# Experts' weights loaded by GpSimd instead of SyncE in an attention and mixture-of-experts kernel

## The chip, the cores and the metric

The kernel runs on one core of a Trainium2 chip. A core has five engines that work side by side, each through its own list of instructions in order: TensorE (PE in the profile; its weight loads are shown apart as PEld), VectorE (DVE), ScalarE (ACT), GpSimd (POOL) and SyncE (SP). Engines wait for each other through semaphores. Transfers between the device memory and the core's buffers are issued by an engine into a DMA queue and carried out by 16 DMA engines. The metric is the device time of one execution in microseconds (us), the median of several runs.

## The reference

Eight sequences of 2496 positions go through an attention without a softmax, then all 19968 tokens through a soft mixture of 8 experts with 4 slots each:

```python
scores = (1/S) * z @ z.T                 # per sequence, S = 2496, z: S x 64
x = u * (maximum(scores, 0)**2 @ v)      # u, v: S x 256
logits = x @ phi                         # 19968 x 32
d = softmax of logits over the tokens
slot_in = d.T @ x                        # 32 slots x 256
slot_out[e] = maximum(slot_in[e] @ w1[e], 0) @ w2[e]   # w1: 8 x 256 x 1024, w2: 8 x 1024 x 256
out = (softmax of logits over the slots) @ slot_out
```

The experts' weights, 16.8 MB in all, are needed only when the slot inputs of all tokens have been summed, that is, after the whole attention.

## The kernel before, in words

**Attention.** The work is a list of 410 "halves" (`halves`, line 209). A half is one block of up to 512 queries against two tiles of 128 keys. For each half the kernel needs the squared scores, split into a rounded part `ph` and its remainder `pl`; three matmuls per pair of tiles then add them into `acc`. Since the score matrix is symmetric, many blocks are not computed again: VectorE transposes a block into `y`, SyncE stores it in device memory (`turned`), and later SyncE fetches it as `r` (`fetch`, line 231). The queries of the last sequence end with a block that is cut in two chunks of 256, so the last 20 halves are half as wide as the others. `weights` (line 599) counts the last 30 halves, 380 to 409.

Where the half three places ahead must be computed (not fetched), `sums_halves` (line 354) runs the current half in two phases on the two row groups of TensorE. Between them stands a hand-over: a no-op on GpSimd waits for the last matmul of phase 0, and the first matmul of phase 1 waits for that no-op. TensorE runs the scores of the half ahead between the phases. The no-op is not an instruction that the profile lists.

**Tokens.** While the attention runs, the token groups of 1024 (`groups`, line 447) are worked off in small pieces, one per half: `logits`, exponentials, and a transposition of the tokens. For the last of these, VectorE turns 32 x 32 blocks (`y`), and 16 small DMAs (`shift`, line 441, four calls of four) move them into place in `xt`. `slot_sums` (line 529; `sl` in the profile) then multiplies `xt` by itself on TensorE: the exponentials against the tokens. The last full group, number 18, has its four shifts and its slot sums among the last halves; the last 512 tokens follow after the attention on a path of their own (lines 744 to 845), which uses two small GpSimd results: line 759 clears part of `tiny`, and line 761 prepares a mask.

**Weights.** 32 loads of 512 KB each (`load_w`, line 594) bring in the experts' weights. `weights(i)` issues loads 0 to 21 in a written order among the last 30 halves, into buffers that the attention no longer needs: 16 that held the split `z` and `v` of the last two sequences, and three that held `y` and `r`. Loads 15, 14, 12, 13, 6, 7, 5, 8, 9, 10 and 11 come in the last ten halves, and each needs a buffer that one of these halves still reads. Loads 22 to 31 (lines 739 to 742) go into space that is free when the attention ends. Layer 1 of the experts reads weights 0 to 15, layer 2 weights 16 to 31.

**Order.** The class `InOrder` (line 51) pins each instruction behind the one traced before it on its engine. TensorE, ScalarE, VectorE and SyncE are used through it. GpSimd is not: a planner orders its instructions by the time at which it reckons them ready, those traced first ahead. The planner also chooses which freed buffer a load takes. A DMA waits in its engine's list until its buffer is free, and all that stands behind it on that engine waits too. DMAs of one issuing path rotate over eight semaphores, and a DMA waits for the one eight places before it to land.

Of the kernel before, what the change touches and what calls it, by code (L numbers as in the profile page):

```python
# [62 lines left out]
def attn_soft_moe_kernel(ctx, tc, uT, v, zz, phi, ww, outT):  # L63
    nc = tc.nc

    pe, act, dve, sp = (InOrder(tc, x) for x in (nc.tensor, nc.scalar, nc.vector, nc.sync))

    def pool(st, name, n, side=None):
        return st.enter_context(
# [522 lines left out]
        w_raw.append(pool.tile([P, 2, 512], F32, tag=tag, name=f"w_{len(w_raw)}"))  # L592

    def load_w(i):
        sp.dma_start(w_raw[i], ww[i].rearrange("p (k n) -> p k n", k=2))

    w_raw = []

    def weights(i):

        if i == 0:
            for _ in range(NBLK):
                take_w(blk, "blk")
        if i == 10:
            for _ in range(3):
                t = turns_sb.tile([P, 16, 4, NS], F32, tag="y", name=f"w_{len(w_raw)}")
                t = t.rearrange("p m i q -> p (m i q)").rearrange("p (a k n) -> p a k n", a=2, k=2)
                w_raw.extend([t[:, 0], t[:, 1]])  # L610
        order = [[], [0], [], [1], [], [2], [], [3], [], [4]]
        order += [[], [16], [17], [], [18], [19], [], [20], [21], []]
        order += [[], [15], [14], [12], [13], [6], [7, 5], [8], [9], [10], [11]]
        for k in order[i]:
            load_w(k)
# [124 lines left out]
    for i in range(NBLK + 6, NW):  # L740
        take_w(wx, "wx")
        load_w(i)

    q = NQG - 1
    x = xg_.pop(q)
# [286 lines left out]
```

## Time and profile before

| | |
|---|---|
| median of 3 runs | 1408.99 us (1407.65 to 1409.12) |
| profiled execution | 1410.43 us, its span 1408.7 us |
| busy share of the span: PE, DVE, ACT, POOL | 97%, 77%, 65%, 0% |
| mean granted TensorE clock | 0.976 |
| DMA queues in use by the kernel | one (q1), 271.02 MB |
| loads of weights | 32 of 512.0 KB, median 7.6 us from issue to landing |

The page is made from one execution. Its numbers are microseconds from the first instruction on, if nothing else is said. A row of a timeline gives start, duration, engine, operation, the tile that is written and those that are read, and how often; in brackets stands the idle time of the engine ahead of it and who ended it. A row of the waits gives who waited for whom, the total, how often and the longest. A row of the stretches gives length, then the busy time and number of instructions of PE, PEld, DVE, ACT and POOL, the granted clock, the DMA share and GB/s; where one engine is asked for, only its own busy time stands there. Nearly all instructions carry line 59, since the helper `InOrder` records them; the tiles' names tell them apart. "SPq" is SyncE's queue of DMA issues. The time of an issue is not that of the transfer.

### The profile page before, as it was taken

What the parts mean: (1) busy time and instruction counts of PE and PEld (TensorE: products, weight loads), DVE (VectorE), ACT (ScalarE), POOL (GpSimd) and SP (SyncE); (2) the same over time, 40 slices, a digit from 0 to 9 for tenths busy, and PEclk for the clock granted to TensorE, in tenths of its full rate; (3) what the DMA queues carried; (4) which work ended last, traced back from release to release, by engine and by line L of the source; (5) the groups of instructions that cost most, each with busy time, mean ns of one, the idle gap of its engine ahead of it and who ended that gap; (6) DMA issues with size and microseconds to landing.
All of it is one profiled execution on the core that took longest, in us unless ns stands there. A gap on an engine that the chain in (4) does not pass through costs nothing.

```text
span 1408.7 us, 27263 instructions
## 1 busy us (share of the span) xinstructions
PE 1362.1 (97%) x11029; PEld 1079.7 (77%) x11029; DVE 1085.8 (77%) x1401; ACT 913.8 (65%) x1046; POOL 4.2 (0%) x22
## 2 busy tenths in 40 slices
PE   9899999999999999899999999899999999999885
PEld 6677887778777887688877888688877788778752
DVE  6778797778888698577987788687888879686454
ACT  7766586757767487465867577474876567664353
POOL 0000000000000000000000000000000000000000
PEclk9999999999999999999999999999999999999985
DMA  4236566394676647576675745748476856659889
GB/s 128 68 109 184 183 154 189 118 290 137 170 233 208 230 111 185 155 214 210 159 211 143 285 138 139 220 127 289 122 189 183 268 160 168 194 149 308 300 329 387
DMA packets 106493, 272.74 MB, mean 194 GB/s; under 512 B 14720, under 2 KB 17280, under 8 KB 95104
## 3 DMA queue, kind: packets, MB, share of 16 engines
q1 hardware_dynamic: 106368, 271.02, 63.6%
q8 instruction: 86, 1.41, 0.4%
q14 instruction: 39, 0.32, 0.1%
HBM read 148.41 MB, written 100.14 MB: 176 GB/s over the span
## 4 chain that ended last, share of the span: by engine, by line
PE 83%; DMA 7%; ACT 3%; DVE 3%; issue 2%; SPq 1%; ACTq 0%; DVEq 0%
PE acc L59 65%; PE sc L59 11%; DMA r<-turned 5%; PE lg L59 3%; PE pf L59 2%; SPq L59 1%; DMA xt<-y 1%; ACT r L59 1%; ACT ot L59 1%; DVE pl L59 1%; ACT ph L59 1%; DVE y L59 1%; PE po L59 1%; PE h L59 1%; DVE xg L59 0%
## 5 line engine op out<-in xcount | busy, mean ns | idle before, releaser
L59 PE MATMUL acc<-ph,v 64*128 64x512 f32 (+5 forms) x5092 | 988.3, 387 | 3.9 <-DVE v L59 1.7
L59 PEld LDWEIGHTS acc<-ph,v 64*128 64x128 f32 (+1 forms) x5092 | 600.6, 186 | 150.7 <-issue 19.7
L59 DVE TENSOR_TENSOR pl<-r,ph 128x1024 fp32r<-128x1024 f32 (+1 forms) x412 | 488.3, 1191 | 196.4 <-ACT ph L59 180.8
L59 PE MATMUL acc<-pl,v 64*128 64x512 f32 (+5 forms) x2546 | 624.5, 384 | 1.8 <-DVE pl L59 1.8
L59 ACT CAST ph<-r 128x1024 fp32r<-128x1024 f32 (+1 forms) x259 | 260.7, 1021 | 204.8 <-DMA r<-turned 130.0
L59 ACT ACTIVATE r<-sc 128x1024 f32<-128x1024 f32 (+1 forms) x252 | 254.9, 1012 | 199.9 <-PE sc L59 192.6
L59 PEld LDWEIGHTS acc<-pl,v 64*128 64x128 f32 (+1 forms) x2546 | 308.4, 185 | 62.5 <-DVE pl L59 4.2
L59 ACT ACTIVATE r<-r 128x1024 f32<-128x1024 f32 (+1 forms) x252 | 263.5, 1047 | 7.2
L59 DVE STREAM_TRANSPOSE y<-r 128x1024 f32<-128x1024 f32 x152 | 188.2, 1238 | 0.0
L59 DVE CAST ph<-r 128x1024 fp32r<-128x1024 f32 (+1 forms) x153 | 102.1, 667 | 57.3 <-ACT r L59 56.6
L59 PE MATMUL sc<-z,z 64*128 64x512 f32 x960 | 138.9, 393 | 2.3 <-DVE z L59 1.4
L59 PEld LDWEIGHTS sc<-z,z 64*128 64x128 f32 x960 | 89.9, 184 | 24.9 <-ACT r L59 2.2
L59 PE MATMUL sc<-z 64*128 64x512 f32 (+1 forms) x480 | 68.4, 390 | 0.0
L59 DVE TENSOR_TENSOR v<-vr,v 128x512 fp32r<-128x512 f32 x80 | 54.0, 675 | 3.7 <-ACT v L59 3.7
L59 DVE TENSOR_TENSOR xg<-acc,ut 128x1024 f32<-128x1024 f32 (+7 forms) x57 | 48.6, 875 | 9.0 <-PE acc L59 9.0
L59 DVE STREAM_TRANSPOSE y<-xg 128x512 f32<-128x512 f32 x76 | 52.6, 692 | 2.5 <-DMA xt<-y 2.5
L59 PEld LDWEIGHTS sc<-z 64*128 64x128 f32 x480 | 45.0, 186 | 8.6
L59 ACT CAST v<-vr 128x512 fp32r<-128x512 f32 x80 | 48.8, 610 | 2.2 <-DMA vr<-in_v 2.2
L59 DVE TENSOR_TENSOR z<-zr,z 64x512 fp32r<-64x512 f32 x70 | 48.1, 687 | 2.0
L59 ACT CAST z<-zr 64x512 fp32r<-64x512 f32 x70 | 43.4, 619 | 2.0 <-DMA zr<-in_zz 0.3
L59 DVE COPY ot<-pf 128x1024 f32<-128x1024 f32 (+2 forms) x22 | 24.3, 1104 | 21.7 <-PE pf L59 21.7
L59 ACT COPY ot<-pf 128x1024 f32<-128x1024 f32 (+2 forms) x22 | 20.1, 915 | 25.6 <-PE pf L59 25.6
(128 smaller groups left out, 417.2 us busy)
## 6 DMA issues: line engine op xcount, KB each, us to landing
turned<-y SPq DMA_DIRECT2D x304, 256.0 KB, 4.3
r<-turned SPq DMA_DIRECT2D x72, 1024.0 KB, 7.7
xt<-y SPq DMA_DIRECT2D x304, 72.0 KB, 3.4
vr<-in_v SPq DMA_DIRECT2D x80, 256.0 KB, 2.9
w<-in_w SPq DMA_DIRECT2D x32, 512.0 KB, 7.6
outT<-ot SPq DMA_DIRECT2D x16, 1024.0 KB, 6.3
ut<-in_uT SPq DMA_DIRECT2D x31, 512.0 KB, 4.3
zr<-in_zz SPq DMA_DIRECT2D x35, 256.0 KB, 7.3
```

Of the source, the lines that this page charges most:

```text
L59: return lambda *a, **k: self.tc.keep_in_program_order(f(*a, **k))
```

## The change

`load_w` issues through GpSimd, by a fifth `InOrder`, and no longer through SyncE. The number, size, written order and destinations of the loads stay as they are, and so does everything else. Being pinned, each load stands behind what was traced before it on GpSimd, no-ops and other loads; the no-ops and lines 759 and 761 are not pinned behind the loads.

```diff
-    pe, act, dve, sp = (InOrder(tc, x) for x in (nc.tensor, nc.scalar, nc.vector, nc.sync))
+    engines = nc.tensor, nc.scalar, nc.vector, nc.sync, nc.gpsimd
+    pe, act, dve, sp, pool_q = (InOrder(tc, x) for x in engines)
...
     def load_w(i):
-        sp.dma_start(w_raw[i], ww[i].rearrange("p (k n) -> p k n", k=2))
+        pool_q.dma_start(w_raw[i], ww[i].rearrange("p (k n) -> p k n", k=2))
```

## The prediction

> **What bounds the kernel now.** I read the page's first part, then who waits for whom around the 32 loads, then the timelines of SyncE and TensorE there.
>
> ```profile
> PE 1362.1 (97%) x11029; PEld 1079.7 (77%) x11029; DVE 1085.8 (77%) x1401; ACT 913.8 (65%) x1046; POOL 4.2 (0%) x22
> ```
>
> TensorE (PE) is busy 97% of the span, so a change of queues can only move its idle time. The loads as a group (ns at least, median, at most; first and last start), and all that TensorE waited for between 1255 and 1350 us (total, times, longest):
>
> ```profile
> L59 SPq DMA_DIRECT2D w<-in_w x32: 327/398/1319, 1263.6 to 1341.1; - x32
> ```
>
> ```profile
> PE sl L59 <- DMA xt<-y: 5.7, 1, 5.7
> PE et_sums L59 <- DVE tiny L59: 0.9, 1, 0.9
> PE h L59 <- ACT tiny L59: 0.3, 1, 0.3
> ```
>
> So no load makes TensorE wait: not the two layers that use the weights, not the attention. What stops it is `sl`, the slot sums of token group 18, for the last of 16 small shifts `xt<-y`. SyncE (SP) issues those; its timeline:
>
> ```profile
> 1307.09 2.41 SPq L59 DMA_DIRECT2D xt<-y  x4
> 1309.60 0.53 SPq L59 DMA_DIRECT2D r<-turned  x1
> 1310.17 5.08 SPq L59 DMA_DIRECT2D xt<-y  x8
> 1315.37 0.52 SPq L59 DMA_DIRECT2D r<-turned  x1
> 1315.99 0.41 SPq L59 DMA_DIRECT2D w<-in_w  x1
> 1316.44 2.41 SPq L59 DMA_DIRECT2D xt<-y  x4
> 1318.95 0.53 SPq L59 DMA_DIRECT2D ut<-in_uT  x1
> 1319.58 21.89 SPq L59 DMA_DIRECT2D w<-in_w  x20
> ```
>
> From 1309.6 to 1319.1 it issues without a gap worth the name, one load (weight 15) directly ahead of the last four shifts and 20 loads behind them. The stall as TensorE shows it, with the attention matmuls around it, and the granted clock (the number behind the busy times), DMA share and GB/s in stretches about it:
>
> ```profile
> 1309.92 0.50 PE L59 MATMUL acc<-ph,v 128*128 128x256 f32 x2
> ...
> 1316.91 0.28 PE L59 MATMUL acc<-pl,v 128*128 128x256 f32 x1
> 1322.85 2.31 PE L59 MATMUL sl<-xt 64*32 64x256 f32 x32 [5.67 <-DMA xt<-y]
> ```
>
> ```profile
> 1317.10:1322.85 5.75, 0.09 (x1) 0.90 1.02 264
> 1322.85:1325.09 2.24, 2.24 (x32) 0.50 1.02 401
> 1325.09:1328.45 3.36, 3.36 (x21) 0.50 1.03 410
> ```
>
> The clock is half from the end of the stall to 1328.45: 2.24 + 3.36 = 5.6 us of work that at the full clock takes 2.8. The mean of 0.90 over the 5.75 us of idling means that the half clock began about a fifth of it, 1.15 us, before its end, some 4.6 us after TensorE stopped. The spot thus costs 5.7 + 2.8 = 8.5 us, all that the change can win here.
>
> **The change part by part.** *SyncE loses 32 issues.* Those before 1307 save nothing: no wait of TensorE stands there, and the first shift at 1307.09 waits for its data. After 1319.58 SyncE has only loads until the output stores. What counts is weight 15: without it the last four shifts are issued 1316.44 - 1315.99 = 0.45 us sooner, and its 512 KB no longer lie ahead of them in the same queue. What a load costs the 16 DMA engines is read where loads run alone, 1325 to 1334:
>
> ```profile
> DMA packets 972, 3.55 MB, mean 394 GB/s; under 512 B 109, under 2 KB 109, under 8 KB 971
> ...
> w<-in_w SPq DMA_DIRECT2D x6, 512.0 KB, 5.8
> ```
>
> 0.524 MB at 394 GB/s is 1.33 us. That this delay is real is seen in the shifts' landing, the four at 1307 against these four:
>
> ```profile
> xt<-y SPq DMA_DIRECT2D x4, 72.0 KB, 2.1
> ```
>
> ```profile
> xt<-y SPq DMA_DIRECT2D x4, 72.0 KB, 5.4
> ```
>
> Removed: 0.45 + 1.33 = **1.8 us**.
>
> *GpSimd (POOL) gains 32 issues, and seven come sooner.* By the code, weights 15, 14, 12, 13, 6, 7, 5 go into buffers that the last chunk's first halves free, one per half, and are pinned behind GpSimd's last hand-over, that of half 400. The whole halves 401 to 405 run from 1309.92 to 1317.19, 1.45 us each. On SyncE these seven queue behind the shifts, and six are issued only from 1319.58. On GpSimd nothing holds them: they go out from about 1309.4 (line 759's memset, shown below, starts right behind that hand-over) to 1317, 7 x 1.33 = 9.3 us of the DMA engines' time, into the stretch in which the shifts and the fetch `r` travel. Room there is in these rows (the last three numbers are clock, DMA share and GB/s):
>
> ```profile
> 1310.00:1316.00 6.00, 6.00 (x52) 6.00 (x53) 4.90 (x10) 3.30 (x7) 0.60 (x2) 1.00 0.73 189
> 1316.00:1323.00 7.00, 1.33 (x12) 1.16 (x11) 3.62 (x9) 1.19 (x3) 0.00 (x0) 0.91 0.95 247
> ```
>
> Idle are 27% of 6.0 and, up to 1322, 5% of 6: 1.6 + 0.3 = 1.9 us. So 9.3 - 1.9 = 7.4 us must be taken from SyncE's transfers or wait behind them. No row shows two queues that compete. Bounds: 0, if SyncE's queue is not held up at all, and 7.4, if the loads always go first. I take the middle, turn and turn about, **3.7 us**, since both queues then have work without a break.
>
> The Trainium skill (DMA: Bandwidth & Descriptors, section Queues, rings and completion order) says that a DMA engine takes turns between the queues that have work, a packet at a time. By that rule the 3.7 stands; where a packet of loads is larger than one of SyncE's, it would be more. No run here shows it yet.
>
> *GpSimd's issue itself.* The trace has no DMA issued there. The nearest row is SyncE's for the same loads: 0.33 us from below, its slowest 1.32 from above. I take 1 us, above the middle, since the engine is another; beyond 1.45 us, one half, loads would pile up (a rival below).
>
> *What is queued behind a load on GpSimd.* First the hand-overs: every half that is computed in two row groups has a no-op on GpSimd between its phases, which waits for TensorE and for which TensorE waits. Those of halves 380 to 382 stand near load 0, those of 395, 396, 399 and 400 near loads 19 to 21. The cover is the scores matmuls between the phases:
>
> ```profile
> 1302.56 0.51 PE L59 MATMUL sc<-z 64*128 64x256 f32 x6
> ...
> 1307.31 0.52 PE L59 MATMUL sc<-z 64*128 64x256 f32 x6
> ```
>
> Loads 20 and 21 follow the hand-over of half 396, at the first of these rows, and have 1307.31 - 1302.56 = 4.75 us until that of half 399, at the second. At 1 us each they are out: cost **0**; if they take longer than 4.75 us, TensorE loses the excess less some 0.4 us of scores. Load 0, after half 380, has a half of 512 columns for itself alone.
>
> Then two small operations for the last token group:
>
> ```profile
> 1309.37 0.73 POOL L759 MEMSET tiny<- 128x512 f32 x1 [1305.65 <-PE acc L59]
> 1310.08 0.52 POOL L761 TENSOR_SCALAR tiny<-ssel 128x128 f32<-128x128 f32 x1
> ...
> 1336.37 0.29 DVE L59 CUSTOM_DVE_ANT_0 tiny<-pm,tiny 128x128 f32<-128x128 f32 x1 [0.20 <-PE et_last L59]
> ```
>
> They are traced after the last load but not pinned to it, and have 1336.37 - 1310.60 = 25.8 us to spare: **0**, if they stay in front of the late loads.
>
> *The late loads.* Weight 11's buffer comes free with the last half:
>
> ```profile
> 1332.70 0.28 PE L59 MATMUL acc<-pl,v 128*128 128x256 f32 x1
> ...
> 1341.22 5.36 PE L59 MATMUL h<-w,tiny 128*32 128x512 f32 x48
> ...
> 1368.77 1.22 PE po L59 x4
> ```
>
> Issued at 1333 and 5.8 us under way, it lands at 1339, and the third of the first layer's four blocks, which reads it, begins a third into the second row, at 1341.22 + 5.36 / 3 = 1343.0: 4 us of cover. Ten more loads at 1.33 us are out by 1347, and weight 31 is read last at 1368.8. **0**; so nothing of the tail moves by itself.
>
> **Sum:** -1.8 + 3.7 = +1.9 us at `sl`; all behind it moves along. The half clock stays, since the stall only grows, from 5.7 to 7.6. The profiled execution took 1410.43 us (span 1408.7 and 1.7 around it), 1.44 above the median of the runs, 1408.99. So 1412.3 on its own count, and **1410.9** against the median; its own range, from the bounds, is -1.8 to +5.6: 1407.2 to 1414.6.
>
> **Rivals.**
>
> *SyncE's queue runs free (faster).* The shifts land 1.8 us sooner, the stall is 3.9 us, below the 4.6 after which the clock halved, and the 2.8 go too: -4.6, **1404.4**. For it: DMA engines idle 27% before 1316. Against: SyncE would have to be served first.
>
> *Stuck behind the loads (slower).* The planner puts line 759's memset and line 761 behind load 31. On SyncE 20 loads took 21.89 us to 1341.5; on GpSimd, likewise bound to the last half and the DMA engines, the memset would begin there and end with its successor at 1342.7, against 1336.37: +6.4 on the chain through the last group, with the 1.9 **1417.3**. It decides as soon as the pair ends after 1336.4. For it: their place in the code. Against: they need only a free buffer, have it early, and in this profile run right after the last hand-over.
>
> *The issue is slow (slower).* At 3 us a load, for instance because GpSimd has to wait for VectorE's (DVE's) copies and casts, of which this is one:
>
> ```profile
> 1309.21 0.43 DVE L59 CAST ph<-r 128x512 fp32r<-128x512 f32 x1 [0.76 <-ACT r L59]
> ```
>
> loads 20 and 21 hold up the hand-over of half 399 by 6 - 4.75 - 0.4 = 0.9 us; the crowd at the shifts is thinner, say half of the 3.7; and the eleventh load from 1309.4, weight 11, is out at 1342.4 and lands 5.8 later at 1348.2, against 1343.0: -1.8 + 1.9 + 0.9 + 5.2 = +6.2, **1415.2**. It decides from about 2.5 us a load. Against: it is over twice SyncE's slowest load, and casts are few there. The Trainium skill (SBUF — State Buffer, section SBUF: two separate sides) warns of just this: a DMA from GpSimd cannot have its descriptors written while VectorE runs a copy in its two-port modes. No run here shows it.
>
> *Only the issue slot.* The transfers end in the order and at the times that they have now, whoever issues them, and the shifts gain the 0.45 us of issue alone: **1408.5**. For it: the loads' data moved at 394 GB/s, so the engines and not SyncE's issue bound them. Against: seven loads are then served no sooner, though asked for sooner. The Trainium skill (DMA: Bandwidth & Descriptors, section Issuing engines are not separate DMA queues) speaks for it and against any real gain: all issuers end on the same 16 engines, and a second one saves only the time to issue.
>
> **How the numbers follow.** Chances: forecast 0.47, SyncE's queue free 0.20, stuck behind the loads 0.11, slow issue 0.07, only the slot 0.15. A measurement of this kernel tells 0.2%, 2.8 us, from nothing: faster is below 1406.2, slower above 1411.8. Faster: nearly all of the second, 0.19. Slower: stuck 0.11, slow issue 0.06, and of the forecast what lies above +2.8 in its -1.8 to +5.6, near two fifths of 0.47, 0.18: 0.35. Same: 0.46. Eight in ten: from 1404.4 (half of the fast rival stays out) to 1415.5 (the stuck rival stays out).
>
> **What would show it.** Right: GpSimd issues seven loads between 1309 and 1318, the wait of `sl` for `xt<-y` stays TensorE's longest after 1255 and is 6.5 to 9 us, the last four shifts are issued near 1316.0 and land more than 6 us later, and the clock is again 0.50 behind it. Wrong: a wait below 4.6 us with the clock near 1.00 (SyncE's queue runs free), a wait of VectorE for line 761 at 1336 (stuck), or a new wait of `acc` for GpSimd, or one of `h` or `po` for `w` (slow issue).

## The result, and the profile after

The changed kernel takes **1422.51 us** (median of 4 runs, 1419.99 to 1425.51) against 1408.99: a ratio of 1.0092, 95% interval 1.0070 to 1.0113. It is 13.5 us slower, and lies above the predicted range. The profiled execution took 1425.51 us (span 1423.7), 15.1 more than that of before. TensorE, VectorE and ScalarE carry out the same instructions in the same order as before, and SyncE the same but for the 32 loads.

Between 1250 and 1380 us TensorE has two long waits: that of `sl` for the shifts, of which the prediction spoke, now about twice as long (10.8 us in two pieces), and a new one of 4.9 us, of `acc` for `pl`. TensorE's timeline of after, with the logits of groups 17 and 18 (`lg`) as landmarks:

```profile
1233.50 1.96 PE L59 MATMUL lg<-xg,phi_sb 64*32 64x256 f32 x32 [1.98 <-DVE xg L59]
...
1302.47 0.58 PE L59 MATMUL acc<-pl,v 128*128 128x256 f32 x1 [4.91 <-DVE pl L59]
...
1307.46 1.59 PE L59 MATMUL lg<-xg,phi_sb 64*32 64x256 f32 x32
...
1337.26 1.03 PE L59 MATMUL sl<-xt 64*32 64x256 f32 x2 [10.28 <-DMA xt<-y]
1338.78 1.96 PE L59 MATMUL sl<-xt 64*32 64x256 f32 x30 [0.48 <-DMA xt<-y]
```

The same landmarks of before (its `sl` starts at 1322.85):

```profile
1233.25 1.10 PE L59 MATMUL lg<-xg,phi_sb 64*32 64x256 f32 x32 [1.84 <-DVE xg L59]
...
1298.20 1.09 PE L59 MATMUL lg<-xg,phi_sb 64*32 64x256 f32 x32
```

They cut the end of the kernel into three stretches, which serve for all runs below: **A** from the logits of group 17 to those of group 18 (before 64.95, after 73.96 us), **B** from there to the first slot sum (24.65 and 29.80), **C** from there to the end of the span (85.85 and 86.44). After loses 9.0, 5.2 and 0.6 us in them.

**Stretch A** holds a stall that was not foreseen. After it the clock is half for the 5.1 us that are left of A, at a cost of 2.55 (and 0.5 more at the start of B, where the logits of group 18 take 1.59 us against 1.09), and after the stall of `sl` it is near half for 5.7 us. Length, TensorE's busy time, granted clock, DMA share and GB/s of these two stretches:

```profile
1302.40:1307.50 5.10, 5.03 (x28) 0.50 0.49 157
...
1337.26:1343.00 5.74, 5.26 (x44) 0.53 0.42 139
```

4.91 + 2.55 = 7.5 us. The other 1.6 of A's 9.0 is no work of the loads: both sets of logits of group 17, some 30 us ahead of the first load, ran at half clock in this execution (the 1.96 above against 1.10). Run 12 below lies 1.65 us above run 11 in A: the loads are the same there, and only 12 has the half clock at these logits. Runs 2, 3, 5 and 7 have it too, at 1.4 to 1.6 us; run 6 does not.

The new stall comes from VectorE, which turns the first block of group 18's tokens into `y`. There is one buffer `y`, and it is free only when group 17's shifts have read it. That wait was there before, with little to spare. VectorE before:

```profile
1292.14 0.71 DVE L59 STREAM_TRANSPOSE y<-xg 128x512 f32<-128x512 f32 x1 [2.53 <-DMA xt<-y]
```

and after:

```profile
1300.00 0.71 DVE L59 STREAM_TRANSPOSE y<-xg 128x512 f32<-128x512 f32 x1 [4.67 <-DMA r<-turned]
```

The second row names a fetch, which this instruction does not read. The chain of the same execution shows what it waited for, the last shift of group 17 (start, time to landing):

```profile
1280.57 14.07 DMA xt<-y
...
1294.66 5.17 DMA xt<-y
```

The shift that SyncE issued at 1280.57 took 14.07 us to land. The last one stands eight places behind it and so could be issued only then, at 1294.66, and took 5.17 us itself. Before, the last shift was issued at 1288.23 and landed 3.7 us later.

From the logits of group 17 to the transposition it is 58.89 us before and 66.50 after: 7.6 later, 6.0 without the 1.6. Of these 6.0 the late issue is 4.6 and the slower landing 1.5. Behind it on VectorE stands the `pl` that TensorE needs; 6.0 - 4.9 = 1.1 us was all the room there was.

Why the shifts are late is seen in who issues when. SyncE before, around the last four shifts of group 17:

```profile
1284.07 0.39 SPq L59 DMA_DIRECT2D w<-in_w  x1
1285.04 3.78 SPq L59 DMA_DIRECT2D xt<-y  x4
1288.92 0.53 SPq L59 DMA_DIRECT2D r<-turned  x1
1289.54 0.88 SPq L59 DMA_DIRECT2D w<-in_w  x2
```

GpSimd and SyncE after:

```profile
1265.46 0.68 POOL L59 DMA_DIRECT2D w<-in_w  x1 [1261.73 <-PE sc L59]
1271.92 2.08 POOL L59 DMA_DIRECT2D w<-in_w  x4 [5.79 <-PE acc L59]
1281.79 1.05 POOL L59 DMA_DIRECT2D w<-in_w  x2 [7.78 <-DVE pl L59]
1284.40 1.05 POOL L59 DMA_DIRECT2D w<-in_w  x2 [1.56 <-DVE pl L59]
```

```profile
1280.57 4.27 SPq L59 DMA_DIRECT2D xt<-y  x4
1287.12 0.34 SPq L59 DMA_DIRECT2D r<-turned  x1
1288.32 6.84 SPq L59 DMA_DIRECT2D xt<-y  x4
```

Before, four loads went ahead of the last four shifts of group 17 and five of the nine behind; after, all nine go ahead, since GpSimd takes them as soon as their buffers are free. And the DMA engines had hardly any room there, before already (clock, DMA share, GB/s at the end; from 1280 to 1285 the share was 0.90):

```profile
1265.00:1270.00 5.00, 5.00 (x46) 1.00 0.99 402
1270.00:1275.00 5.00, 5.00 (x29) 1.00 0.99 365
1275.00:1280.00 5.00, 5.00 (x23) 1.00 0.98 269
```

Five loads by the 1.33 us that the prediction read off are 6.7 us, an estimate, against the 6.0 by which `y` is late. SyncE's transfers issued between 1265 and 1292 (number, KB, median us to landing), before:

```profile
w<-in_w SPq DMA_DIRECT2D x5, 512.0 KB, 7.0
r<-turned SPq DMA_DIRECT2D x4, 512.0 KB, 6.0
...
xt<-y SPq DMA_DIRECT2D x12, 72.0 KB, 6.2
```

and after:

```profile
r<-turned SPq DMA_DIRECT2D x3, 512.0 KB, 11.7
...
xt<-y SPq DMA_DIRECT2D x10, 72.0 KB, 11.2
```

The fetches `r` are late as well, and a second stall lies hidden behind the first. The `ph` that belongs to the late `pl` was ready at 1295.1, so TensorE stood for the transposition alone; but ScalarE could begin the cast of the next half only at 1298.96, after 3.82 us of waiting for `r`. Without the late shifts TensorE would have stopped there instead, by an estimate from these rows for one to two us.

**Stretch B** is the foreseen place: GpSimd issues weights 15 to 5 ahead of group 18's last shifts, all seven before SyncE issues the last four shifts. GpSimd:

```profile
1319.61 1.05 POOL L59 DMA_DIRECT2D w<-in_w  x2 [5.28 <-PE sc L59]
...
1327.28 0.53 POOL L59 DMA_DIRECT2D w<-in_w  x1 [0.87 <-PE acc L59]
```

and SyncE:

```profile
1328.00 2.95 SPq L59 DMA_DIRECT2D xt<-y  x4
```

The chain has the same two steps as in A, one shift late and then the last, which had to wait for it:

```profile
1322.95 7.48 DMA xt<-y
...
1330.44 8.29 DMA xt<-y
```

Of B's 5.15 us the longer wait of `sl` is 4.6, and 0.5 is the end of A's half clock.

### The profile page after: what moved, and what is told of

It reads as the page before. It is cut to its first block, busy times and chain, and to the rows that moved or that the text cites. A ratio compares the mean times of both kernels' runs of the same rounds, so it can differ in the third digit from the quotient of the medians.

```text
span 1423.7 us, 27280 instructions
## 1 busy us (share of the span) xinstructions
PE 1366.3 (96%) x11029; PEld 1081.2 (76%) x11029; DVE 1085.5 (76%) x1401; ACT 913.1 (64%) x1046; POOL 20.7 (1%) x54
## 2 busy tenths in 40 slices
DMA packets 106494, 272.75 MB, mean 192 GB/s; under 512 B 14720, under 2 KB 17280, under 8 KB 95104
## 4 chain that ended last, share of the span: by engine, by line
PE 80%; DMA 9%; ACT 4%; DVE 3%; issue 2%; SPq 1%; DVEq 0%; ACTq 0%
PE acc L59 62%; PE sc L59 11%; DMA r<-turned 5%; DMA xt<-y 4%; PE lg L59 3%; ACT r L59 2%; PE pf L59 1%; DVE pl L59 1%; ACT ph L59 1%; ACT ot L59 1%; SPq L59 1%; DVE y L59 1%; PE po L59 1%; DVE xg L59 1%; DMA outT<-ot 1%
```

## The experiments

The theory after the result: the loads cost time only by the bytes that they put into the DMA engines ahead of shifts that are waited for, nine loads in A and seven in B. The table gives all kernels; A, B and C come from each profiled execution by the three landmarks. The kernel before was run again beside each group, at 1409.4 to 1409.9.

| kernel | median us | ratio (95%) | A | B | C |
|---|---|---|---|---|---|
| before | 1408.99 | | 64.95 | 24.65 | 85.85 |
| after | 1422.51 | 1.0092 (1.0070 to 1.0113) | 73.96 | 29.80 | 86.44 |
| 1 first nine on SyncE | 1416.63 | 1.0047 (1.0034 to 1.0061) | 64.94 | 28.79 | 87.94 |
| 2 only these nine on GpSimd | 1416.97 | 1.0054 (1.0033 to 1.0074) | 73.14 | 25.25 | 85.50 |
| 3 eleven wait for the sums | 1415.29 | 1.0044 (1.0027 to 1.0062) | 72.72 | 23.63 | 86.42 |
| 4 before, load 15 later | 1408.47 | 0.9991 (0.9976 to 1.0006) | 64.95 | 22.80 | 84.96 |
| 5 nine early on SyncE | 1417.49 | 1.0058 (1.0040 to 1.0076) | 75.11 | 25.02 | 85.95 |
| 6 nine early on ScalarE | 1416.79 | 1.0049 (1.0034 to 1.0064) | 71.44 | 25.48 | 85.83 |
| 7 loads cut in two | 1422.40 | 1.0089 (1.0073 to 1.0105) | 73.90 | 29.40 | 86.26 |
| 8 all on GpSimd, paced | 1409.63 | 1.0003 (0.9990 to 1.0015) | 64.95 | 23.44 | 88.62 |
| 9 and shifts shared | 1405.56 | 0.9975 (0.9963 to 0.9987) | 64.95 | 19.53 | 88.18 |
| 10 four shifts shared | 1407.53 | 0.9984 (0.9974 to 0.9995) | 64.95 | 19.46 | 88.88 |
| 11 as 9, nine loads first | 1404.79 | 0.9963 (0.9951 to 0.9976) | 64.95 | 19.63 | 85.85 |
| 12 as 11, eleven not held | 1418.79 | 1.0060 (1.0046 to 1.0074) | 66.60 | 20.50 | 97.63 |

### 1 and 2: one part of the change alone

```diff
-        pool_q.dma_start(w_raw[i], ww[i].rearrange("p (k n) -> p k n", k=2))
+        q = sp if i in (0, 1, 2, 3, 4, 16, 17, 18, 19) else pool_q
+        q.dma_start(w_raw[i], ww[i].rearrange("p (k n) -> p k n", k=2))
```

The second has `pool_q` and `sp` the other way round.

> Loads 0 to 4 and 16 to 19 go by SyncE again, the other 23 stay on GpSimd. Theory (the loads on the second queue crowd out SyncE's small shifts, at two separate places): the wait of acc for pl near 1300, 4.9 us, and the half clock behind it go, the wait of sl for the shifts stays near 10 us: about 1414.5 us. Rival (a price of GpSimd's issue itself, paid per load): 23 of 32 loads keep 23/32 of the 13.5 us: 1418.7. Rival (the first place doesn't matter): no change, 1422.5.

> The reverse: loads 0 to 4 and 16 to 19 on GpSimd, the other 23 on SyncE. Theory: the wait of acc for pl near 1300 with its half clock stays (about 7.7 us), the wait of sl is again about 5.7 us: 1416.7. Rival (a price per load): 9 of 32, 3.8 us: 1412.8.

With the first nine on SyncE the new stall is gone and the sums wait as in the changed kernel; with only these nine on GpSimd it is the other way round. TensorE's stalls of 1:

```profile
1324.96 1.03 PE L59 MATMUL sl<-xt 64*32 64x256 f32 x2 [9.70 <-DMA xt<-y]
```

and of 2:

```profile
1301.65 0.58 PE L59 MATMUL acc<-pl,v 128*128 128x256 f32 x1 [4.87 <-DVE pl L59]
...
1331.10 2.59 PE L59 MATMUL sl<-xt 64*32 64x256 f32 x32 [6.16 <-DMA xt<-y]
```

Their losses, 7.0 and 7.3 us against 1409.68, add up to 14.2, the changed kernel's 13.5 within its interval (9.9 to 15.9). So these are two separate costs of about the same size, and no third is needed. The time of 1 alone lies between the theory's 1414.5 and the 1418.7 of a price per load; C is 2.1 us longer there, with the clock at half for 7.5 us behind the stall. Run 2 decides: by a price per load it would take 1412.8, and it takes 1416.97.

### 3: the eleven late loads wait for the slot sums

```diff
-        pool_q.dma_start(w_raw[i], ww[i].rearrange("p (k n) -> p k n", k=2))
+        d = pool_q.dma_start(w_raw[i], ww[i].rearrange("p (k n) -> p k n", k=2))
+        if sums_done and i < 16:
+            await_(d, sums_done[-1])
...
-        order += [[], [15], [14], [12], [13], [6], [7, 5], [8], [9], [10], [11]]
+        order += [[], [], [], [], [], [], [], [15, 14, 12, 13, 6, 7, 5, 8], [9], [10], [11]]
```

> All loads on GpSimd, but 15, 14, 12, 13, 6, 7, 5, 8, 9, 10, 11 wait for the slot sums of group 18. No load is then under way with that group's shifts. Theory: the wait of sl falls to 3.9 us or less and the clock isn't halved behind it, the first stall stays: 1408.99 + 7.7 - 4.6 = 1412.1. Rival (the shifts are slow because GpSimd's queue is in use at all, or the price is per load): sl keeps 10 us, 1422.5.

```profile
1299.93 0.58 PE L59 MATMUL acc<-pl,v 128*128 128x256 f32 x1 [4.55 <-DVE pl L59]
...
1327.68 2.19 PE L59 MATMUL sl<-xt 64*32 64x256 f32 x32 [4.54 <-DMA ut<-in_uT]
```

The sums wait 4.5 us (the profile names `ut`, which SyncE issues behind the last shifts), less than the 5.7 of before; B is 1.0 shorter than before. So the seven loads alone cause the second loss. A keeps the first: it is 7.8 us longer than before, 1.6 of it at the logits of group 17. The theory's 1412.1 was too low by 3.2 us: the wait stayed 0.6 us above the 3.9 that it allowed, and the clock was half again behind it (2.19 us for 32 matmuls), where it had counted on saving 2.8 us. The side is the theory's and not the rival's.

### 4: the kernel before, load 15 behind the last shifts

```diff
-        order += [[], [15], [14], [12], [13], [6], [7, 5], [8], [9], [10], [11]]
+        order += [[], [], [15, 14], [12], [13], [6], [7, 5], [8], [9], [10], [11]]
```

> The kernel before, all loads on SyncE, with load 15 one half later, behind the last four shifts. The prediction's term of 1.8 us (0.45 of issue, 1.33 of data ahead in the queue): the wait of sl falls from 5.7 to 3.9 us, the clock isn't halved, 1404.4. If the clock stays halved: 1407.2. Rival (load 15 wasn't what the shifts waited for): 1409.0.

This is the prediction's removed term by itself.

```profile
1321.84 1.76 PE L59 MATMUL sl<-xt 64*32 64x256 f32 x32 [3.71 <-DMA xt<-y]
```

The wait falls from 5.67 to 3.71, by 1.96 us, and B by 1.85, where 1.8 had been worked out. The clock fell to half all the same, if for a shorter time (1.76 us for the 32 matmuls, 2.31 before), so the 4.6 us of idling that the prediction read off for it are no limit. The median fell by 1.2 us, which the interval does not tell from nothing.

### 5 and 6: early, but not on GpSimd

```diff
-        if i == 10:
+        if i == 6:
...
-        order = [[], [0], [], [1], [], [2], [], [3], [], [4]]
-        order += [[], [16], [17], [], [18], [19], [], [20], [21], []]
+        order = [[], [0], [], [1, 2, 3, 4], [], [], [16, 17], [18, 19], [], []]
+        order += [[], [], [], [], [], [], [], [20], [21], []]
```

Both start from the kernel before. The first line takes the buffers of loads 16 to 21 four halves sooner. In 6 `load_w` also issues these nine through `act`.

> Kernel before, but the nine loads 0 to 4 and 16 to 19 stand in SyncE's own queue at the early places at which GpSimd took them; GpSimd issues nothing. Theory (what counts is how many loads go ahead of group 17's shifts, on whichever queue): a new stall of about 5 us ahead of a sum of the chunk before the logits, as in the run with these nine on GpSimd, and a time near 1417, 1414 to 1419. Rival (two queues taking turns are the cause, one queue in order is not): no such stall, 1409.7 as before.

> The same nine loads at the same early places, issued by ScalarE on its hardware queue, the other 23 on SyncE. Theory (early loads, whichever queue): the new stall of about 5 us, near 1417. Rival (something of GpSimd's software queue alone): no stall, 1409.7. The nine issues stand in ScalarE's own order, some 0.5 us each, so up to 2 us more by that.

Both lose what 2 loses. TensorE and then SyncE in 5:

```profile
1299.14 0.58 PE L59 MATMUL acc<-pl,v 128*128 128x256 f32 x1 [6.03 <-DVE pl L59]
```

```profile
1264.48 3.37 SPq L59 DMA_DIRECT2D w<-in_w  x4
1267.90 5.03 SPq L59 DMA_DIRECT2D xt<-y  x4
```

In 6 the same stall is 3.99 us, and in 5 the last shift of group 17 took 7.4 us to land, 3.7 before. So neither GpSimd nor a second queue is the cause: in 5 there is one queue, as before, and the loads only stand further ahead in it. It is the order in which the transfers are asked for.

### 7: each load as two transfers

```diff
-        pool_q.dma_start(w_raw[i], ww[i].rearrange("p (k n) -> p k n", k=2))
+        for k in range(2):
+            pool_q.dma_start(w_raw[i][:, k], ww[i][:, k * 512 : (k + 1) * 512])
```

> The changed kernel with each load as two transfers of 128 rows of 2 KB instead of one of 128 rows of 4 KB; the bytes are the same. Rival (the two queues take turns packet by packet, so half the packet takes half as much from the shifts): both stalls shrink, the longest wait of the sums from 10.3 to about 8 us, 1416. Theory (the loads' bytes go ahead of the shifts, whatever their cut): both stalls stay, 1422.5; GpSimd issues 64 transfers, at 0.53 us each 17 us more of its time, which is hidden.

Nothing changed, 1422.40 us. But this leaves open whether the size of a packet counts. GpSimd's queue before the cut (packets, MB, share), in the changed kernel:

```profile
q0 software_dynamic: 4608, 16.78, 3.4%
```

and in 7:

```profile
q0 software_dynamic: 5120, 16.78, 3.5%
```

512 packets more, and the page counts 512 more under 512 B in the whole execution (15232 against 14720): the packets that carry the data are as many and as large as before. It does show that twice as many issues on GpSimd cost nothing here.

### 8: all loads on GpSimd, held back by what is to go first

```diff
+        if sums_done:
+            await_(d, sums_done[-1])
+        else:
+            await_(d, turned_18[0])
...
+        order = [[]] * 13 + [[0, 1, 2, 3, 4, 16, 17]] + [[]] * 13
+        order += [[15, 14, 12, 13, 6, 7, 5, 8], [9], [10], [11, 18, 19, 20, 21]]
```

`turned_18[0]` is VectorE's first transposition of group 18, the one that waits for group 17's shifts.

> The changed kernel, all 32 loads on GpSimd, held back: loads 0 to 4, 16 and 17 wait until VectorE's first block of group 18 is turned (group 17's shifts have landed by then), the other loads up to 21 wait for the slot sums of group 18. Theory (only loads that go ahead of shifts cost time): no new stall, the sums wait 3.7 to 5.7 us, 1408.5 to 1410, the time before. Rival (a second queue costs time in itself, or GpSimd's does): 1415 or more.

GpSimd's loads in 8:

```profile
1287.45 3.87 POOL L59 DMA_DIRECT2D w<-in_w  x7 [1283.72 <-DVE y L59]
1320.71 4.23 POOL L59 DMA_DIRECT2D w<-in_w  x8 [13.57 <-PE sl L59]
```

A is 64.95 to the hundredth, as in the kernel before, B 23.44, the time 1409.63: the loss is gone to within 0.15%, with all 32 loads on GpSimd's queue. That is the theory, shown from the other side. C is 2.8 us longer than before, of which 1.6 is a wait of the experts' second layer (`po`) for weights that were asked for late.

### 9, 10 and 11: what a second queue is good for

In 8 nothing but shifts is ahead of the last shifts, and still the sums wait 4.45 us: SyncE needs 0.6 us for each of the sixteen. So some go to GpSimd, which is free then: eight in 9, four in 10.

```diff
-            sp.dma_start(xt[32 * b : 32 * b + 32, a], src[32 * a : 32 * a + 32, b])
+            queue.dma_start(xt[32 * b : 32 * b + 32, a], src[32 * a : 32 * a + 32, b])
...
+        shifts = [lambda a=a: shift(y(), a, pool_q if q == NQG - 2 and a > 1 else sp) for a in range(4)]
```

> The kernel with the paced loads on GpSimd, and of group 18's sixteen shifts the last eight on GpSimd's queue as well, which is idle then. Theory (with no load ahead of them the last shifts are late only because SyncE issues sixteen of them one after the other, 0.6 us each from 1307 on): all are issued some 5 us sooner, the sums wait 0 to 1.5 us instead of 4.5, TensorE's clock isn't halved, and the time is 1402 to 1405. Rival (the landing, not the issue, is what is waited for, and GpSimd's queue lands later: 9.8 us for a load against 7.6): 1408 to 1412.

> The same, with the last four shifts of group 18 alone on GpSimd, behind the last hand-over of a half on that engine. Theory: SyncE issues twelve, the last 2.4 us sooner than before; the sums wait 1.5 to 3 us, 1405 to 1407. Rival: 1408 to 1412.

GpSimd in 9, then TensorE:

```profile
1305.51 4.24 POOL L59 DMA_DIRECT2D xt<-y  x8 [13.44 <-DVE slot_acc L59]
```

```profile
1315.02 1.09 PE L59 MATMUL sl<-xt 64*32 64x256 f32 x32
```

The sums wait for nothing and run at full clock (32 matmuls in 1.09 us, 2.31 before). B falls to 19.5 in both, 5.1 below before. In 10 the sums wait 0.47 us, less than the 1.5 to 3 expected, and yet it takes longer than the 1405 to 1407; its C is 3.0 us longer than before. Run 9 lies just above its 1402 to 1405. Part of what 9 could have won is lost in C, which is 2.3 us longer than before. The experts wait 2.4 us for late weights, as TensorE's waits in 9 show:

```profile
PE po L59 <- DMA w<-in_w: 1.6, 3, 0.8
...
PE h L59 <- DMA w<-in_w: 0.8, 2, 0.5
```

11 moves loads 18 and 19 to the first seven:

```diff
-        order = [[]] * 13 + [[0, 1, 2, 3, 4, 16, 17]] + [[]] * 13
+        order = [[]] * 13 + [[0, 1, 2, 3, 4, 16, 17, 18, 19]] + [[]] * 13
```

> The kernel with shared shifts, but nine loads instead of seven (18 and 19 too) go in the gap after group 17's shifts. Theory (behind the sums, the experts now wait for late weights, 2.4 us of waits for loads in the run before this): 1 MB less to fetch behind the sums, so the waits for loads shrink by 1 to 2 us and the time is 1403.5 to 1405. Rival (the extra loads reach into group 18's shifts, which begin 1304): the sums wait 1 to 3 us again, 1406 to 1409.

C falls to 85.85, the time to **1404.79**, ratio 0.9963 (0.9951 to 0.9976): 5.1 us below the 1409.93 of the kernel before beside it, the lowest of all.

### 12: the eleven loads not held back

```diff
-        if sums_done:
-            await_(d, sums_done[-1])
-        else:
+        if i in (0, 1, 2, 3, 4, 16, 17, 18, 19):
             await_(d, turned_18[0])
...
+        order += [[15, 14], [12], [13], [6], [7, 5], [8], [9], [10], [11, 20, 21]]
```

> As the last, and the eleven loads from 15 on don't wait for the slot sums any more: they stand on GpSimd behind its eight shifts and go as their buffers come free. Theory (a load costs only where it goes ahead of a shift that is waited for, and these go behind): the sums wait 0 to 1 us, the waits for loads go, 1402 to 1404. Rival (loads that run beside the last shifts slow them though they were issued later): the sums wait 2 to 4 us, 1406 to 1409.

The sums wait 1.3 us in two pieces, a little over the theory's 0 to 1 and below the rival's 2 to 4: loads issued behind the shifts hardly touch them. Yet the time is 1418.79, outside both, from a cause that neither named. GpSimd and TensorE in 12:

```profile
1341.19 0.53 POOL L59 DMA_DIRECT2D w<-in_w  x1 [0.75 <-DMA w<-in_w]
1341.71 0.55 POOL L765 MEMSET tiny<- 128x512 f32 x1
1342.21 0.32 POOL L767 TENSOR_SCALAR tiny<-ssel 128x128 f32<-128x128 f32 x1
```

```profile
1343.51 0.64 PE L59 MATMUL lg_last<-tiny,slot_acc 128*128 128x32 f32 x2 [11.73 <-DVE tiny L59]
```

The planner put the memset and the mask behind the last of the 32 loads, and the last group waits 11.7 us for them (C 97.63). This is the prediction's rival "stuck behind the loads", which the changed kernel had escaped.

## Why the prediction was wrong

- **"Those before 1307 save nothing: no wait of TensorE stands there."** True of the issues that SyncE loses, and wrong as the whole account of these loads. Nothing was charged for what they do on GpSimd's side, where they run ahead of group 17's shifts. This step failed, and the term left out is the larger: 7.5 us in the changed kernel, 7.3 in run 2. The sign was to be had from the trace of before: VectorE waits there 2.53 us for these shifts, the DMA engines are 98% to 99% busy, and five loads times 1.33 gives 6.7 against a measured 6.0. That only 1.1 us could be lost before TensorE felt it is known from the changed kernel. The prediction looked only where TensorE already waited.
- **"Turn and turn about, 3.7 us."** Mis-sized. The wait grew by 4.6 us, and with the 1.8 that is saved the added term is 6.4; in run 1, where the first nine loads are back on SyncE, 4.1 + 1.8 = 5.9. Both lie nearer the upper bound of 7.4 than the middle. The working had one delay, of the last four shifts; the trace has two in a row, since an earlier shift landed late and the last was issued only behind it. The Trainium skill (DMA: Bandwidth & Descriptors, section Queues, rings and completion order) has the DMA engines take turns between queues; whether they do so here, no run tells. The stall in A was longer in run 5, in one queue, than in 2 and 6, in two (6.03 us against 4.87 and 3.99), which is the direction of turns, but the loads don't stand at quite the same places.
- **"The half clock stays", 2.8 us of cost.** Nearly: C grew by 0.6 us in the changed kernel, 0.5 of it a second wait of the sums, and by 2.1 in run 1. The new stall in A brought a half clock of its own, about 3 us with its end in B.
- **Removed, 0.45 + 1.33 = 1.8 us.** Right; run 4 measured 1.96 in the wait.
- **GpSimd's issue, 1 us.** 0.53 measured, half; it changed nothing. The rival of a slow issue falls with it: issues took 0.53 us with VectorE at work beside them, and in run 7, where one of its casts ran beside them, six took 3.28 us.
- **Hand-overs 0, late loads 0, lines 759 and 761 0.** Right in the changed kernel: no wait of `acc` for GpSimd, none of `h` or `po` for `w`. The last hung on the planner alone, as run 12 shows.
- **The seven loads from 1309 to 1318 and the wait of 6.5 to 9 us.** They came, later by the first stall, at 1319.6 to 1327.8; the wait was 10.3 and 0.5. The last four shifts did not keep their place: they went out 20.5 us after the logits of group 18, 18.2 before.

Put together with what was measured, 1409.0 + 7.5 + 5.2 + 0.6 = 1422.3, against 1422.51. The Trainium skill (DMA: Bandwidth & Descriptors, section Issuing engines are not separate DMA queues) says that a second issuer saves only issue time, since all transfers end on the same 16 engines. The traces agree, with their numbers: sharing the shifts saved SyncE eight issues and did away with a wait of 4.45 us (runs 8 and 9), while moving the loads saves one issue of 0.45 us where it counts. The 13.5 us come from something else: a queue that lets go earlier than the old one reorders the traffic.

One thing stays open, the packet-by-packet share of two queues. Where 11 lost part of its gain is in the trace. Without the half clock its C should be 2.8 us shorter than before, 83.05, and it is 85.85. The sums themselves lack 0.4 of it (1.47 us for 32 matmuls, not 1.09). The experts' first layer takes 9.36 us from the first `h` to the first `hT` against 7.71 before, 1.65 more, since TensorE's loads of weights into its array (PEld) wait for late weights, between 1330 and 1342 us (total, times, longest):

```profile
PEld h L59 <- DMA w<-in_w: 2.1, 3, 1.5
```

And from the end of TensorE's last matmul to the end of the span, when only the output is on its way, it is 8.98 us against 8.04.

## What to carry to other kernels

An in-order DMA queue is also a schedule: what stands behind something in it is thereby given lower priority. Before a group of transfers is moved to another queue, ask for each one when that queue will let it go, whether the DMA engines have room at that moment, and which small transfer somebody waits for then, through other engines too and not only where the bounding engine stalls today. Move the small, urgent transfers to the idle queue rather than the large ones, and tie the large ones to an event behind the urgent ones; and give each operation behind many loads on an in-order engine its place by hand.

## What the runs showed of the hardware

- One late landing holds up later issues. Four shifts took SyncE 2.4 us where there was room, 4.27 and 6.84 in the changed kernel in stretch A, and yet each issue took 0.51 to 0.82 us (0.51 to 0.61 before). The rest is waiting for earlier transfers to land, one of them for 14.07 us.
- A DMA issue of 512 KB took GpSimd 0.53 us, SyncE 0.40 in the median.
- The clock did not halve by a fixed length of the pause. After 1.98 us of waiting, group 17's logits ran at half clock in the changed kernel (1.96 us for 32 matmuls, first row of its timeline above); after 2.33 us, in run 1, at the full clock (1.10 us).
